# Activations' operands begin 0 to 128 bytes further into their places, by turns: linear attention and two squared-ReLU networks on one core

## The chip, the core and the metric

One core of a Trainium2 chip runs the whole program. The metric is device time in microseconds. The profile is of one execution; its times are us from the span's start.

## The reference, cut to what matters

```
q, k, v: 8 x 8 heads x 576 x 64
q_s = softmax(q) over the 64 features;  k_s = softmax(k) over the 576 positions
kv = k_s^T v  per head;   x = q_s kv    -> 4608 tokens x 512
for each of two networks (w_in 512 x 2048, w_out 2048 x 512):
    h = max(x @ w_in, 0);   x = (h * h) @ w_out
```

## The kernel before, in words

The tokens are worked in nine blocks j of 512; the 2048 hidden features are 16 blocks f of 128 (NF), or 8 pairs a (NPAIR), or 4 groups u of two pairs (NU). Every operand of a large matmul is kept as two halves of float32r, a high one and a low one (what the rounding left), and each product is three matmuls in a row, low x high, high x low, high x high: `passes`, line 460. Each matmul has a stationary operand of 128 columns, which is loaded anew for it, and a moving one of 512 or 256 columns.

There are four stages, one after the other:

1. The first network's first product, "h" (`h_mm`): 1728 matmuls of 512 columns. The weight w0 is stationary, the token block's x moving. Attention is done beside it: `attend(j, p)` for each of four pairs of heads p makes kv and x. x goes from the bank to memory in `x_hi` (L79, ScalarE, high half) and `x_lo` (L82, VectorE, low half). The result is taken out by `h_relu` (L447, ScalarE) and stored to HBM. A block of tokens is 16 hidden blocks of 12 matmuls, in order of the pair of heads c = 0 to 3, three matmuls for each.
2. Its second product, "y<-G,W" (`second`, l=0): 72 pairs (j, a) of 42 matmuls of 256 columns; G, the squared hidden values, is moving and the weight W stationary. Products are done in a form with 7 instead of 8 block products, whose operands are sums of blocks: `combine` makes them, by adds on VectorE or GpSimd (L100 to L104), the high half in `comb_hi` (L114, ScalarE) and the low half in `comb_lo` (L119, VectorE).
3. The second network's first product, "m<-x,W" (`first`): 36 units (j, u) of 84 matmuls; x moving, W stationary.
4. Its second product, "y<-W,G" (`second`, l=1): as stage 2, but W moving and G stationary.

Places in on-chip memory are laid out by hand, by `room` at the top, in the order of the calls; a room takes its words of four bytes, and at least 32 bytes. The rooms w0 to w7 hold the combined weights (14 x 256 words each), the rooms hl0 to hl3 the combined x and G; in the first stage w0 to w4 hold the weights w0 (three to a room, 1024 words each), hl0 and hl1 the x of even and odd token blocks for the pairs of heads 0 to 2, at words 1024 p, and hl3 ("ahead") holds the weight of hidden block 15 at word 0 and the x of pair 3 at word 1024 for even and 2048 for odd blocks. G of the last stage (names G1_...) begins SHIFT = 32 words into its place. At the start, the data of two pairs of heads lie in one room, 1738 words apart (`start_load`), and their transposes (`k_turn0`, `q_turn0`) take them as the stationary operand.

The order of all instructions on each engine comes from a planner (`schedule`) with costs and due times, which knows places by name and not by address; the eight banks of "ps" are given out in the order in which they come free. Waits between engines are added where the addresses that one instruction writes overlap what another reads or writes.

Of the kernel before, what the change touches and what calls it, by code (L numbers as in the profile page):

```python
# [16 lines left out]
B, H, S, D = 8, 8, 576, 64  # L17
# [4 lines left out]
NP = H // 2  # L22
TB = 512
HB = TB // 2
NB = NT // TB
NF = DFF // P
NPAIR = NF // 2
# [3 lines left out]
SHIFT = 32  # L31
# [12 lines left out]
def linear_attention_two_relu2_ffn(ctx: ExitStack, tc: tile.TileContext, q0, k0, eye, qh, kh, vh, wio, out):  # L44
# [15 lines left out]
    def room(tag, n):  # L60
        pool.tile([P, n], F32, name=f"{tag}_room", tag=tag)

    for i in range(8):
        room(f"w{i}", 14 * HB)
    for tag, n in (("kvn", D), ("qm", 16), ("qs", 16), ("qmo", 16)):
        room(tag, n)
    room("hl3", 14 * HB)
    room("hl0", 14 * HB + SHIFT)
    for tag, n in (("qso", 16), ("kvs", 1), ("kvm", 1), ("margin0", 64)):
        room(tag, n)  # L70
    room("hl1", 14 * HB + SHIFT)
    room("margin1", 96)
    room("hl2", 14 * HB + SHIFT)

    def f32(ap):
        return ap.bitcast(F32)
# [14 lines left out]
    hls, cfs = {}, {}  # L91


    def comb_add(key, q, x, eng, new):
# [8 lines left out]
        else:  # L103
            e.tensor_tensor(out=cf[:, 4], in0=q[:, 0], in1=q[:, 3], op=ALU.add)  # L104

    def comb_hi(key, q, x, tag):
        if key not in hls:
            if key.startswith("G1_"):
                t = pool.tile([P, 14 * HB + SHIFT], F32R, name=key, tag=tag)
                hls[key] = t[:, SHIFT:].rearrange("p (a b n) -> p a b n", a=2, b=7)  # L110
            else:
                hls[key] = pool.tile([P, 2, 7, HB], F32R, name=key, tag=tag)
        r, src = (slice(0, 2), q[:, 0:4:3]) if x == 0 else (slice(2, 7), cfs[key])
        nc.scalar.activation(out=hls[key][:, 0, r], in_=src, func=AF.Copy)  # L114
# [223 lines left out]
    kvn = {}  # L338
# [25 lines left out]
    qmo, qso = {}, {}  # L364
# [104 lines left out]
    m, t, t_place = {}, {}, {}  # L469
# [235 lines left out]
    def combine(key, tag, due, engines, q, place, after, cfplace, new):  # L705

        hl = Place(tag)
        n = (512, 512, 256)
        adds = [op(e, gps(n[x]) if e == "POOL" else dve(n[x]), due - 5200 + 10 * x, lambda x=x, e=e: comb_add(key, q(), x, e, new), after, [place, cfplace], port=True)
                for x, e in enumerate(engines)]  # L710
        h0 = op("ACT", act(512), due - 4500, lambda: comb_hi(key, q(), 0, tag), after, [hl, place])
        h1 = op("ACT", act(1280), due - 3000, lambda: comb_hi(key, q(), 1, tag), adds, [hl, cfplace])
        l0 = op("DVE", dve(512), due - 2500, lambda: comb_lo(key, q(), 0), [h0], [hl, place], port=True)
        l1 = op("DVE", dve(1280), due - 1500, lambda: comb_lo(key, q(), 1), [h1], [hl, cfplace], port=True)
        combined[key] = [l0, l1], hl
# [50 lines left out]
    ahead = Place("hl3")  # L766
# [94 lines left out]
    xspace = [Place("hl0"), Place("hl1")]  # L861

    def attend(j, p):
# [3 lines left out]
        if j == 0:  # L867
            room = start_places[p]
        kvnew = lambda: kp.area(0, KC * (P + 2 * (D + 1)))
        qnew = lambda: qspace.area(TB * (p % 2), TB)  # L870
        if own:
            ps = Place("ps")
            n, s = Place("kvn"), Place("kvs")
# [33 lines left out]
        else:  # L907
            q = Place(f"q{p % 2}", parent=qspace)
            lq = dma(d - 30000, lambda: load_q(j, p, qnew), 256, [], [q])
            qm, qo, qs, so, qT, qd = Place("qm"), Place("qmo"), Place("qs"), Place("qso"), Place("qT"), Place("qd")  # L910
# [15 lines left out]
                kv_ready[p] = op("DVE", 450, d - 5500, lambda: kv_lo(j, p), [hi], [n, kvp[p]], port=True)  # L926
                xlast = op("PE", 60 + 3 * 29 * (8 - j), d - 4500, lambda: x_mm(j, p, 1, xb), [kv_ready[p], xm], [xb, qd, kvp[p]], lag=SLACK)
        par = j % 2
        room2, lo = (ahead, 1024 * (1 + par)) if p == NP - 1 else (xspace[par], 1024 * p)
        xp = x_place[j, p] = Place(f"x{par}_{p}", parent=room2)  # L930
        y = op("ACT", act(512, 1), d - 2000, lambda: x_hi(j, p, lambda: part2(room2, lo)), [xlast], [xp, xb])
        x_ready[j, p] = op("DVE", dve(512), d - 1000, lambda: x_lo(j, p), [y], [xp, xb])
# [1 line left out]
    for j in range(NB):  # L934
        for p in range(NP):
            plan(when(0, j) - 25000 - (3 - p) * 12500, lambda j=j, p=p: attend(j, p))
# [246 lines left out]
```

## Time and profile before

| | |
|---|---|
| median of 3 runs | 1572.17 us (1571.39, 1572.17, 1589.4) |
| profiled execution | 1568.28 us, its span 1566.5 us |
| TensorE busy / weight loads busy | 1529.8 / 1428.7 us |
| VectorE, ScalarE, GpSimd busy | 1203.2, 957.8, 418.1 us |
| mean granted clock of TensorE | 0.992 |

The span is from the first to the last instruction. Matmuls overlap in the records: one of 256 columns lasts 276 to 281 ns, while the next begins some 115 ns after it. So the pace of a stretch is its length, less the last one's own duration where that is in it, by the number of intervals.

### The profile page before, as it was taken

The page shows a single profiled execution, that of the slowest core. Times are in us where ns is not written, and L with a number is a line of the kernel's source. Part 1 is how long each engine was busy: PE and PEld are TensorE (multiplying, and loading weights), DVE is VectorE, ACT ScalarE, POOL GpSimd, SP SyncE. Part 2 cuts the span into 40 slices and gives each one's busy share as a digit, 9 for nine tenths or more (in the row PEclk, how much of TensorE's full clock was granted, in tenths as well). Part 3 has the DMA queues.
Part 4 walks back from the last instruction along what each step waited for, and adds up shares of the span by engine and source line. Part 5 has one row for each costly group of instructions (what it writes and reads, how often), then busy time and mean ns, then how long its engine had stood idle before and what let it go on. Part 6 is the DMA issues. An engine that isn't in the chain of part 4 may idle for free.

```text
span 1566.5 us, 30005 instructions
## 1 busy us (share of the span) xinstructions
PE 1529.8 (98%) x11664; PEld 1428.7 (91%) x11664; DVE 1203.2 (77%) x1758; ACT 957.8 (61%) x1605; POOL 418.1 (27%) x337
## 2 busy tenths in 40 slices
PE   6899999999999999999999999999999899999998
PEld 4678878878888999999999999999999899999998
DVE  7897887778744888888889855555445898999987
ACT  7666765667655655555555788888777444444442
POOL 1010000000013233333323444333321433334332
PEclk9899999999999999999999999999999999999999
DMA  8447766778685444444437667767648544444432
GB/s 327 155 140 219 252 226 211 230 266 274 242 293 178 139 146 134 135 135 136 135 109 250 239 213 248 242 224 241 209 169 292 206 137 146 136 142 141 136 118 85
DMA packets 143103, 299.86 MB, mean 191 GB/s; under 512 B 12528, under 2 KB 72048, under 8 KB 141424
## 3 DMA queue, kind: packets, MB, share of 16 engines
q1 hardware_dynamic: 141808, 283.26, 54.4%
q0 software_dynamic: 1152, 14.68, 2.5%
q8 instruction: 91, 1.49, 0.4%
q14 instruction: 52, 0.43, 0.1%
HBM read 176.26 MB, written 121.63 MB: 190 GB/s over the span
## 4 chain that ended last, share of the span: by engine, by line
PE 91%; DVE 3%; DMA 2%; ACT 2%; issue 1%; POOL 0%; SPq 0%; DVEq 0%; ACTq 0%; POOLq 0%
PE y L460 42%; PE h L460 25%; PE m L460 20%; PE kvps L329 2%; DMA g<-t 1%; DMA hl<-g 1%; PE xps L422 1%; PE xps L423 1%; PE xps L424 1%; DVE G L119 0%; DMA w<-k 0%; DMA raw<-wio 0%; ACT w L147 0%; DVE w L82 0%; POOL att L104 0%
## 5 line engine op out<-in xcount | busy, mean ns | idle before, releaser
L460 PE MATMUL h<-hl,w 128*128 128x512 f32 x1620 | 402.2, 403 | 10.2 <-DVE w L82 10.2
L460 PEld LDWEIGHTS h<-hl,w 128*128 128x128 f32 x1620 | 305.6, 191 | 83.9 <-DVE w L82 9.6
L460 PE MATMUL y<-G,W 128*128 128x256 f32 x3024 | 356.5, 281 | 1.1 <-DVE G L119 1.1
L460 PEld LDWEIGHTS y<-G,W 128*128 128x128 f32 x3024 | 356.3, 189 | 1.3 <-DVE G L119 1.3
L460 PE MATMUL y<-W,G 128*128 128x256 f32 x3024 | 346.1, 277 | 4.1 <-DVE G L119 4.1
L460 PEld LDWEIGHTS y<-W,G 128*128 128x128 f32 x3024 | 345.5, 189 | 4.5 <-DVE G L119 4.5
L460 PE MATMUL m<-x,W 128*128 128x256 f32 x3024 | 343.5, 276 | 0.1
L460 PEld LDWEIGHTS m<-x,W 128*128 128x128 f32 x3024 | 343.1, 188 | 0.3 <-ACT ts L493 0.3
L114 ACT ACTIVATE G<-hl 128x512 fp32r<-128x512 f32 (+1 forms) x106 | 93.1, 889 | 139.2 <-PE y L460 82.6
L119 DVE TENSOR_TENSOR G<-hl,G 128x512 fp32r<-128x512 f32 (+1 forms) x106 | 129.6, 1228 | 20.4 <-ACT G L114 20.4
L447 ACT ACTIVATE r<-h 128x512 f32<-128x512 f32 x144 | 85.6, 595 | 84.2 <-PE h L460 79.1
L496 POOL TENSOR_TENSOR ts<-ts,ts 128x512 f32<-128x512 f32 x53 | 83.3, 1571 | 160.2 <-ACT ts L493 156.2
L314 POOL PARTITION_ALL_REDUCE m<-m x28 | 25.4, 908 | 348.2 <-DVE m L310 168.9
L511 ACT ACTIVATE t<-t 128x512 f32<-128x512 f32 x144 | 90.2, 631 | 3.6
L119 DVE TENSOR_TENSOR G<-cf,G 128x1280 fp32r<-128x1280 f32 x51 | 85.9, 1683 | 6.3 <-ACT G L114 6.3
L505 DVE TENSOR_TENSOR t<-m,ts 128x512 f32<-128x512 f32 x72 | 48.7, 688 | 53.0 <-PE m L460 36.8
L119 DVE TENSOR_TENSOR G<-att,G 128x1280 fp32r<-128x1280 f32 x50 | 81.8, 1637 | 7.6 <-ACT G L114 7.5
L114 ACT ACTIVATE G<-qc 128x512 fp32r<-128x512 f32 x41 | 25.9, 632 | 79.1 <-PE y L460 65.5
L114 ACT ACTIVATE G<-qd 128x512 fp32r<-128x512 f32 x40 | 25.3, 632 | 79.1 <-PE y L460 51.7
L114 ACT ACTIVATE G<-att 128x1280 fp32r<-128x1280 f32 x50 | 63.3, 1266 | 15.2 <-DVE att L102 12.0
L114 ACT ACTIVATE G<-cf 128x1280 fp32r<-128x1280 f32 x51 | 64.6, 1266 | 11.4 <-DVE cf L102 8.2
L538 POOL TENSOR_TENSOR t<-t,t 128x512 f32<-128x512 f32 x34 | 62.5, 1859 | 30.1 <-DVE t L505 30.1
(175 smaller groups left out, 1977.4 us busy)
## 6 DMA issues: line engine op xcount, KB each, us to landing
g<-r SPq DMA_DIRECT2D x144, 256.0 KB, 3.4
g<-t SPq DMA_DIRECT2D x144, 256.0 KB, 3.5
hl<-g SPq DMA_DIRECT2D x63, 512.0 KB, 3.7
raw<-wio SPq DMA_DIRECT2D x48, 512.0 KB, 5.0
qc<-g SPq DMA_DIRECT2D x41, 512.0 KB, 3.8
qd<-g SPq DMA_DIRECT2D x40, 512.0 KB, 3.7
y<-t SPq DMA_DIRECT2D x72, 256.0 KB, 2.3
W<-o POOLq DMA_DIRECT2D x8, 1792.0 KB, 9.7
```

Of the source, the lines that this page charges most:

```text
L114: nc.scalar.activation(out=hls[key][:, 0, r], in_=src, func=AF.Copy)
L119: nc.vector.tensor_tensor(out=hl[:, 1, r], in0=src, in1=f32(hl[:, 0, r]), op=ALU.subtract)
L314: nc.gpsimd.partition_all_reduce(m[:, 1, :P], m[:, 0, :P], P, bass.bass_isa.ReduceOp.max)
L329: nc.tensor.matmul(ps[j * D:(j + 1) * D, 0:D + 1], k[lo:, c, j * D:(j + 1) * D], v[lo:, c, j, :], start=(c == 0), stop=(c == KC - 1),)
L422: nc.tensor.matmul(ps[:, r], w[:, 1], q[:, 0, r], start=True, stop=False)
L423: nc.tensor.matmul(ps[:, r], w[:, 0], q[:, 1, r], start=False, stop=False)
L447: nc.scalar.activation(out=r0[j, f].rearrange("p a b -> p (a b)"), in_=m.pop(("h", j, f)), func=AF.Relu)
L460: nc.tensor.matmul(ps, a, b, start=start, stop=True, skip_group_check=True)
L496: nc.gpsimd.tensor_tensor(out=t[k, "s5"], in0=t[k, "s5"], in1=t[k, "s2"], op=ALU.add)
L505: nc.vector.tensor_tensor(out=temp(k, q), in0=m[k, i], in1=t[k, "s5"], op=ALU.add)
L511: nc.scalar.activation(out=t[k, q], in_=t[k, q], func=AF.Square)
L538: nc.gpsimd.tensor_tensor(out=t[k, q], in0=t[k, q], in1=t[k, o], op=ALU.add)
```

## The change

The moving and stationary operands that are made of x and G no longer all begin at the start of their places (or 32 words in, for G1). A new function `further` gives the words: for G of layer l, token block j, pair a it is 4 x ((8 j + a) modulo 9), for x{j}_{kk} of the second network 4 x j, and the first stage's x begins 4 j words further too. So the starts go through 0, 16, ... 128 bytes. The weights' places stay. The rooms hl0 to hl3 all have 32 words more than the operand needs, and the small rooms between them are laid out anew, so that the hl rooms lie 14592 bytes apart; kvn has no room of its own at this point any more and comes later.

```diff
-    for tag, n in (("kvn", D), ("qm", 16), ("qs", 16), ("qmo", 16)):
+    for tag, n in (("qm", 16), ("qs", 16), ("kvs", 1)):
         room(tag, n)
-    room("hl3", 14 * HB)
-    room("hl0", 14 * HB + SHIFT)
-    for tag, n in (("qso", 16), ("kvs", 1), ("kvm", 1), ("margin0", 64)):
-        room(tag, n)
-    room("hl1", 14 * HB + SHIFT)
-    room("margin1", 96)
-    room("hl2", 14 * HB + SHIFT)
+    for i, between in ((3, (("qmo", 16), ("qso", 16))), (0, (("kvm", 1), ("margin0", 24))), (1, (("margin1", 32),)), (2, ())):
+        room(f"hl{i}", 14 * HB + SHIFT)
+        for tag, n in between:
+            room(tag, n)
...
+    def further(key):
+
+        n = [int(x) for x in key[1:].split("_")]
+        return 4 * ((n[1] * NPAIR + n[2]) % 9 if key[0] == "G" else n[0])
+
     def comb_hi(key, q, x, tag):
         if key not in hls:
-            if key.startswith("G1_"):
+            if key[0] in "Gx":
                 t = pool.tile([P, 14 * HB + SHIFT], F32R, name=key, tag=tag)
-                hls[key] = t[:, SHIFT:].rearrange("p (a b n) -> p a b n", a=2, b=7)
+                o = further(key)
+                hls[key] = t[:, o:o + 14 * HB].rearrange("p (a b n) -> p a b n", a=2, b=7)
...
-        room2, lo = (ahead, 1024 * (1 + par)) if p == NP - 1 else (xspace[par], 1024 * p)
+        room2, lo = (ahead, 1024 * (1 + par) + 4 * j) if p == NP - 1 else (xspace[par], 1024 * p + 4 * j)
```

## Rows read from the trace of the kernel before

**Rows 1.** The page's busy times: engine, us, share of the span, instructions.

```profile
PE 1529.8 (98%) x11664; PEld 1428.7 (91%) x11664; DVE 1203.2 (77%) x1758; ACT 957.8 (61%) x1605; POOL 418.1 (27%) x337
```

**Rows 2.** The page's chain that ended last: shares by engine, by line.

```profile
PE 91%; DVE 3%; DMA 2%; ACT 2%; issue 1%; POOL 0%; SPq 0%; DVEq 0%; ACTq 0%; POOLq 0%
PE y L460 42%; PE h L460 25%; PE m L460 20%; PE kvps L329 2%; DMA g<-t 1%; DMA hl<-g 1%; PE xps L422 1%; PE xps L423 1%; PE xps L424 1%; DVE G L119 0%; DMA w<-k 0%; DMA raw<-wio 0%; ACT w L147 0%; DVE w L82 0%; POOL att L104 0%
```

**Rows 3.** The same chain in order of time: start, length, engine, count.

```profile
457.54 53.10 PE h L460 x228
510.64 336.39 PE y L460 x2856
...
872.23 315.82 PE m L460 x2784
...
1235.32 323.58 PE y L460 x2838
```

**Rows 4.** Windows, line 460: length, PE and PEld busy (count), clock, DMA.

```profile
520.00:840.00 320.00, 320.00 (x2719) 320.00 (x2718) 1.00 0.41 134
...
1240.00:1540.00 300.00, 300.00 (x2649) 300.00 (x2648) 1.00 0.41 133
...
468.00:507.00 39.00, 39.00 (x168) 31.42 (x168) 1.00 0.62 193
```

**Rows 5.** Timeline of PE around the pause at 863 us.

```profile
855.33 5.82 PE L460 MATMUL y<-G,W 128*128 128x256 f32 x48
...
865.13 2.66 PE L460 MATMUL y<-G,W 128*128 128x256 f32 x22
```

**Rows 6.** Timeline of PE, beginning of the last stage.

```profile
1208.28 2.99 PE L460 MATMUL y<-W,G 128*128 128x256 f32 x24
```

**Rows 7.** Timeline of PE, end of the first stage.

```profile
507.73 2.23 PE L460 MATMUL h<-hl,hl 128*128 128x512 f32 x9
509.80 0.84 PE L460 MATMUL h<-hl 128*128 128x512 f32 x3
510.48 0.28 PE L460 MATMUL y<-G,W 128*128 128x256 f32 x1
```

**Rows 8.** Timeline of PE, q times kv of block 4.

```profile
244.72 0.28 PE L422 MATMUL xps<-qhl,kvbd 128*128 128x256 f32 x1
244.84 0.28 PE L423 MATMUL xps<-qhl,kvbd 128*128 128x256 f32 x1
```

**Rows 9.** Timeline of PE, transposes of the start, pairs 2 and 3.

```profile
15.31 0.60 PE L273 MATMUL ka<-begin,w 128*128 128x128 f32 x4
...
16.71 0.60 PE L273 MATMUL ka<-begin,w 128*128 128x128 f32 x4
```

**Rows 10.** Timeline of several engines around the ends of blocks 3, 5, 7.

```profile
259.80 0.69 DVE L82 TENSOR_TENSOR hl<-xps,hl 128x512 fp32r<-128x512 f32 x1
260.81 2.73 PE L460 MATMUL h<-hl,w 128*128 128x512 f32 x11
...
363.65 0.69 DVE L82 TENSOR_TENSOR hl<-xps,hl 128x512 fp32r<-128x512 f32 x1 [0.28 <-ACT hl L79]
365.43 0.40 PE L460 MATMUL h<-hl,w 128*128 128x512 f32 x1
...
458.21 0.69 DVE L82 TENSOR_TENSOR hl<-xps,hl 128x512 fp32r<-128x512 f32 x1
460.92 1.26 ACT L114 ACTIVATE S<-cf 128x1280 fp32r<-128x1280 f32 x1
465.73 3.67 PE L460 MATMUL h<-hl,w 128*128 128x512 f32 x15
```

**Rows 11.** The page's groups and DMA issues that write or read activations.

```profile
L114 ACT ACTIVATE G<-qc 128x512 fp32r<-128x512 f32 x41 | 25.9, 632 | 79.1 <-PE y L460 65.5
...
hl<-g SPq DMA_DIRECT2D x63, 512.0 KB, 3.7
...
qc<-g SPq DMA_DIRECT2D x41, 512.0 KB, 3.8
```

## The prediction, made before the result was known

> **What bounds the kernel now.** I read the page's busy table first: TensorE is busy 98% of the span, and the weight loader 91% beside it [rows 1]. The chain of work that ended last says the same from the other side: 91% of the span is TensorE, 87% the three matmul groups of the two networks, and no wait of another engine takes more than about 1% [rows 2]. So only two things can move the time: the interval from one matmul to the next, and a wait that newly reaches TensorE. VectorE and ScalarE at 77% and 61% are cover.
>
> The interval is then to be read stage by stage, from unbroken stretches of the chain [rows 3], since the table of groups gives mean durations that overlap. It is the length divided by the count: 53.10/228 = 232.9 ns for the 512-column matmuls of the first network's first product (h), 336.39/2856 = 117.8 ns for its second product (y, 256 columns), 315.82/2784 = 113.4 ns for the second network's first (m), 323.58/2838 = 114.0 ns for its second. The granted clock is 1.00 in the stretches looked at [rows 4], its 2.4 GHz level, so one column per cycle would be 213.3 and 106.7 ns. All lie above that, and two stages with the same shape differ by 4 ns without a clock to explain it.
>
> The useful view is the timeline of TensorE around pauses. At 855 us y<-G,W runs at (5.82-0.28)/47 = 117.9 ns (0.28 is the last one's own duration, the last row of [rows 7] shows one alone). After a pause near 863 the very same product runs at (2.66-0.28)/21 = 113.3 [rows 5]. Then m keeps the fast one (its 113.4) for over 300 us; the next stage starts at 1208 us with (2.99-0.28)/23 = 117.8, and from 1240 us it holds 300/2649 = 113.3 [rows 3, 4, 6]. So 256-column matmuls with the same relation of addresses have two stable paces, about 113.3 and 117.8, entered by chance after a disturbance and held for hundreds of us. In this profile y got the slow one, m and nearly all of the last stage the fast one. The three times of the kernel spread by 18 us; one stage in the other pace is 3024 x 4.5 ns = 13.6 us, which is the right size.
>
> Does the address matter at all? One place speaks for it. From the layout, all weights of the stages begin on one residue modulo 512 bytes, and each moving or stationary activation so that the weight-side operand lies 64 bytes ahead (modulo 512): the room hl3 begins 448 bytes (modulo 512) behind the weights' room, the spacings between the hl rooms are multiples of 512, and G of the last stage, there the stationary one, has the extra 128. Only the weight w0 of hidden block 15 lies in hl3 itself, with distance 0 from x. There h runs at 226.7 ns: three matmuls from 509.80 until the next stage starts at 510.48 [rows 7], against 232.9 beside it. It isn't clean: the nine before these take (2.23-0.39)/8 = 230, as if the pace settled over some matmuls. In 4 and 8 ns steps, then, relative position seems to matter, and 113.3 and 226.7 (17/16 of a cycle per column) look like the floor.
>
> **The change part by part.** No instruction is added, removed or reordered, so I cost four things.
>
> (1) *New relations.* The hl rooms now begin 160 bytes behind the weights modulo 256, and each operand 16k further, k from 0 to 8. The stationary operand's lead over the moving one, 64 before, becomes 96-16k (96 down to -32, modulo 256) in the first three stages, and -96+16k in the last. x has k = j through a whole token block; G of the second products has a new k for each of the 72 pairs of hidden blocks. No row shows any lead but 64, 0 and those of a few short products, so this is bounded. From below by the floor: 113.3 and 226.7. From above by the slow pace that lasts, 117.8, and for h by 232.9. Further away, 256-column matmuls of the q times kv product (distance 0) follow one another at 120 ns [rows 8], but these come three at a time after other work; I take 120 as the far end alone. Between floor and slow pace I take the middle, 115.6 and 229.8: nothing in the rows prefers one end, each was entered from a restart, and nine relations in turn make it unlikely that a stage stays in one.
> - y: 3024 x (115.6-117.8) = -6.7 us
> - m: 3024 x (115.6-113.4) = +6.7 us
> - last stage: 3024 x (115.6-114.0) = +4.8 us
> - h: 1728 x (229.8-232.9) = -5.4 us
>
> Sum -0.6 us.
>
> The Trainium skill, in "TensorE: Matmul & The Clock Gate" (Part 2, Step-by-step: what each phase is for), says that TensorE has two independent read ports, so that loading the next weights takes nothing from the running matmul. By it the relation of addresses would be worth nothing and (1) would be 0 instead of -0.6 us; the 226.7 beside 232.9 is against it, weakly, and it is a rival below.
>
> (2) *Starts that are no multiple of 64 bytes.* The transposes of the start are such a case, with the data as the stationary operand: in one room pair 3's k lies 6952 bytes (40 modulo 64) behind pair 2's, and groups of four take 0.60 us for both, (0.60-0.27)/3 = 110 ns an interval [rows 9]. So an unaligned start of weights costs under 1 ns. For a moving operand I see no row at full pace; 0, at most 1 ns on 10,800 matmuls (11 us, inside the bounds of (1)).
>
> (3) *A new wait.* The x of head pair 3 lies in hl3 at word 1024+4j for even j and 2048+4j for odd j. For even j the end of its low half at 2048+4j now covers the first four words of the previous block's x, at 2048+4(j-1). So x_lo (L82, VectorE) has to wait for the last matmul of block j-1. For j=2 that had ended anyway. For j=4 it ran at 259.80 and the next block began at 260.81; for j=6 at 363.65 against 365.43; for j=8 at 458.21 against 465.73 [rows 10]. VectorE will stand 1.0, 1.8 and 7.5 us. Behind it at j=8 are adds for a weight that is kept, and ScalarE's conversion of their sums (460.92) then holds back h_relu, which empties TensorE's banks. I cost it at nothing: x_lo's 0.69 us end by 466.5, and the matmul that reads it is the eleventh of the block, 10 x 0.233 us after its start, at 468.1; ScalarE is held some 7 us, or three hidden blocks at 2.8 us, and there are eight banks, handed out in turn; the next product starts only at 510. Without that cover it costs the waits themselves, 10.3 us together.
>
> (4) *Other engines.* Their operands move too, by whole 16 bytes. I take nothing: their work lies beside TensorE, with ScalarE idle for longer before its conversions of G (79.1 us in 41) than they take (25.9), and loads into hl land in 3.7 us, into qc in 3.8 [rows 11], 20 us ahead of use. A loss of 5% on these would still be covered.
>
> The profiled run took 1568.28 us, 3.9 below the median of 1572.17. Its sum gives 1567.7; on the median, 1571.6.
>
> **The rivals.**
> - *All released to the floor* (the slow pace is a lock that needs a fixed relation; changing it by turns breaks it). y 3024 x 4.5 = 13.6, h 1728 x 6.2 = 10.7, the others 2.4: 26.7 us, so 1546. For: the pause at 863 cleared it, and distance 0 gave the floor in h. Against: at 1208 the fast pace was lost as easily.
> - *Slow throughout, the other side* (each turn of the relation knocks the matmuls into 117.8). m +13.3, last stage +11.5: 1597, and 1600 with part of (3). It decides from the point where more than half of the 256-column matmuls run slow. For: the changes from fast to slow around 1208. Against: there matmuls of two products alternated, and G's changes come only every 42.
> - *Slower than any lasting pace shown*: 256 columns at 120, h 3.1 ns above its 232.9: 9072 x (120-115.1) + 1728 x 3.1 = 50 us, 1622. For: rows 8. Against: no long stretch does that.
> - *The change does nothing*: pace is TensorE's own, entered by chance. Then the middle of before, 1572, with its own spread up to 1589.
> - *The 17/16 goes too*: 9072 x 6.6 + 1728 x 13.4 = 83 us below the floor case at most, half of it 1505. Against: it is the same at distance 0 and 64.
>
> **How the numbers follow.** The forecast (a mixture) has 0.47; a quarter to three quarters slow gives +-10.1 us for the 256s and +-2.7 for h, 1559 to 1585. Released 0.15, slow throughout 0.20, slower than shown 0.10, nothing 0.05, floor gone 0.03. The time is the mixture's, 1571. Its range reaches to 1546 and to 1600, the bounds of (1), and leaves out the two far cases, 0.13. Two per cent, about what a measurement here can tell from no change, is 31 us: faster only with the floor gone, 0.03; slower with 120 ns, or slow with every wait of (3) uncovered (1607), 0.12; the rest 0.85.
>
> **What would show it.** In the chain of the changed kernel: the mean interval of each stage, against 115.6, 115.6, 115.6 and 229.8; in windows by token block, steps of h and m with j (one relation each), which would prove that address and not chance sets the pace; stretches of hundreds of us at one pace across many k would prove the rival that nothing hangs on it. On VectorE, x_lo of blocks 4, 6 and 8 ending 0.7 us after the block boundary, and no pause of TensorE behind it. The prediction is wrong if some leads cost much more than 4.5 ns, or if TensorE pauses near 466 us.

## The result, and the profile after

The changed kernel takes 1594.95 us, median of 4 runs (1594.16 to 1596.04), against 1575.25 for the kernel before in the same job; the ratio is 1.0113, 95% interval 1.0066 to 1.0159. It is slower, by less than the 2% bound and by more than the interval. It lies inside the range, 24 us above the forecast, at the rival "slow throughout" (1597). The profiled execution took 1596.04 us, its span 1594.2, so 27.7 more than the span before.

The page first: busy table, then the chain that ended last, by engine (answers to rows 1 and 2).

```profile
PE 1556.9 (98%) x11664; PEld 1454.8 (91%) x11664; DVE 1204.2 (76%) x1758; ACT 957.8 (60%) x1605; POOL 415.5 (26%) x337
...
PE 76%; DVE 1%; DMA 1%; POOL 1%; issue 1%; ACT 0%; DVEq 0%; POOLq 0%; ACTq 0%; SPq 0%
```

TensorE gained 27.1 us of busy time with the same 11664 matmuls; the other engines moved by less than 3 us, and the mean granted clock is 0.992 in both executions. (In this trace the chain couldn't be followed back over the first 300 us; the shares add to 80%.) So the time is in the matmuls themselves. The chain in order of time says in which (start, length, what; answers to rows 3):

```profile
331.58 5.67 PE h L463 x24
...
397.29 5.47 PE h L463 x24
...
457.79 53.11 PE h L463 x228
510.90 331.82 PE y L463 x2814
...
869.51 353.35 PE m L463 x3000
...
1249.56 337.08 PE y L463 x2838
```

| stage | ns a matmul before [rows 3] | after | forecast |
|---|---|---|---|
| h, 512 columns | 232.9 | 53.11/228 = 232.9 (last blocks) | 229.8 |
| y | 117.8 | 331.82/2814 = 117.9 | 115.6 |
| m | 113.4 | 353.35/3000 = 117.8 | 115.6 |
| last | 114.0 | 337.08/2838 = 118.8 | 115.6 |

By these rates m costs 3024 x 4.4 = 13.3 us more and the last stage 3024 x 4.8 = 14.5. The starts of the stages in the two traces (y 510.48 and 510.74, m 867.85 and 869.35, last stage 1208.28 and 1222.69) share the 27.7 out exactly: 0.3 before y, 1.2 in y, 12.9 in m, 13.3 from the last stage on, which had run its first matmuls at 117.8 before the change too [rows 6].

The lead is how far the stationary operand's start lies ahead of the moving one's, modulo 256 bytes. The first two rows of h show that blocks with different leads do differ: 236 ns in block 5 (lead 16), 228 in block 6 (lead 0).

The view that tells most is the timeline of TensorE inside m, where each token block has one lead for about 40 us. Rows: start, length, group, count; the interval is (length - 0.28)/(count - 1).

```profile
874.74 27.50 PE L463 MATMUL m<-x,W 128*128 128x256 f32 x233
...
911.79 30.45 PE L463 MATMUL m<-x,W 128*128 128x256 f32 x254
...
956.83 25.44 PE L463 MATMUL m<-x,W 128*128 128x256 f32 x223
...
991.75 30.43 PE L463 MATMUL m<-x,W 128*128 128x256 f32 x254
...
1071.82 30.39 PE L463 MATMUL m<-x,W 128*128 128x256 f32 x258
...
1111.77 30.40 PE L463 MATMUL m<-x,W 128*128 128x256 f32 x252
...
1151.80 30.42 PE L463 MATMUL m<-x,W 128*128 128x256 f32 x255
```

Block 0, lead 96: 117.3 ns. Block 1, lead 80: 119.2. Block 2, lead 64: 113.3. Block 3, lead 48: 119.2. Block 5, lead 16: 117.2. Block 6, lead 0: 120.0. Block 7, lead -16: 118.6. (Blocks 4 and 8, leads 32 and -32, ran at 118.3 and 116.7.) One of the nine relations is as fast as before, the one that the kernel before had everywhere; the others all cost 3 to 7 ns. The short turns of y repeat it (last three rows: pairs at leads 80, 64, 48 of token block 2, 119.5, 113.1, 119.2). But not every turn at lead 64 was fast: of its eight in y, one (first row, token block 1) stayed at 117.8 to its end.

```profile
565.49 4.52 PE L463 MATMUL y<-G,W 128*128 128x256 f32 x37
...
605.23 4.82 PE L463 MATMUL y<-G,W 128*128 128x256 f32 x39
...
610.71 4.24 PE L463 MATMUL y<-G,W 128*128 128x256 f32 x36
...
615.02 4.81 PE L463 MATMUL y<-G,W 128*128 128x256 f32 x39
```

The new wait, in the timeline of VectorE and TensorE at the ends of blocks 3, 5 and 7 (answers to rows 10; in brackets the idle time before and its releaser):

```profile
259.90 2.27 PE L463 MATMUL h<-hl,w 128*128 128x512 f32 x9
260.17 0.69 DVE L79 TENSOR_TENSOR hl<-xps,hl 128x512 fp32r<-128x512 f32 x1 [0.93 <-PE h L463]
...
366.64 1.54 PE L463 MATMUL h<-hl,w 128*128 128x512 f32 x6
366.91 0.69 DVE L79 TENSOR_TENSOR hl<-xps,hl 128x512 fp32r<-128x512 f32 x1 [3.36 <-PE h L463]
...
460.68 0.69 DVE L79 TENSOR_TENSOR hl<-xps,hl 128x512 fp32r<-128x512 f32 x1 [2.36 <-PE h L463]
465.96 0.85 PE L463 MATMUL h<-hl,w 128*128 128x512 f32 x3
```

VectorE stands 0.9, 3.4 and 2.4 us, and TensorE goes from block to block without a pause, as costed. The third one is let go 5 us before the block's end: x_lo of block 8 stands in the program ahead of block 7's hidden blocks 14 and 15, so it waits for 13 alone. Those two hidden blocks then read four columns of block 7's x (pair of heads 3, high half) that already hold block 8's; the changed kernel computes that part of four tokens otherwise than the reference, and so do the runs below that keep this place of x (lead 0 fixed, lead 64 fixed, h alone). It changes no duration.

### The profile page after: what moved, and what is told of

Its sections match the earlier page's. It is cut to its first block, busy times and chain, and to the rows that moved or that the text cites. A ratio compares the mean times of both kernels' runs of the same rounds, so it can differ in the third digit from the quotient of the medians.

```text
span 1594.2 us, 30008 instructions
## 1 busy us (share of the span) xinstructions
PE 1556.9 (98%) x11664; PEld 1454.8 (91%) x11664; DVE 1204.2 (76%) x1758; ACT 957.8 (60%) x1605; POOL 415.5 (26%) x337
## 4 chain that ended last, share of the span: by engine, by line
PE 76%; DVE 1%; DMA 1%; POOL 1%; issue 1%; ACT 0%; DVEq 0%; POOLq 0%; ACTq 0%; SPq 0%
PE y L463 43%; PE m L463 22%; PE h L463 10%; DMA qc<-g 0%; PE kvps L332 0%; DVE G L122 0%; DMA hl<-g 0%; POOL cf L101 0%; ACT G L117 0%; POOL att L101 0%; PE xps L426 0%; PE xps L427 0%; PE xps L425 0%; ACT qc L457 0%; DVEq L1182 0%
## 5 line engine op out<-in xcount | busy, mean ns | idle before, releaser
L463 PE MATMUL y<-W,G 128*128 128x256 f32 x3024 | 359.8, 281 | 3.8 <-DVE G L122 3.8
L463 PEld LDWEIGHTS y<-W,G 128*128 128x128 f32 x3024 | 359.1, 189 | 4.2 <-DVE G L122 4.2
L463 PE MATMUL m<-x,W 128*128 128x256 f32 x3024 | 356.6, 280 | 0.0
L463 PEld LDWEIGHTS m<-x,W 128*128 128x128 f32 x3024 | 356.4, 189 | 0.0
```

The lines of the kernel that those rows point to most:

```text
L463: nc.tensor.matmul(ps, a, b, start=start, stop=True, skip_group_check=True)
```

## The experiments

Theory: the value of the lead, modulo 256, sets the pace (the interval between matmuls), at lead 64 with two possible paces. Rivals: that the turning costs (each new relation disturbs the lock), that starts off a multiple of 64 bytes cost, or that only the lead modulo 128 counts. One thing no run separates for y, m and the last stage: the weights there always begin on one residue, so "lead" could also be read as the place of the activation's own start. Only in h did the weights move.

**One lead for y and m: 0, then 64.**

```diff
-        return 4 * ((n[1] * NPAIR + n[2]) % 9 if key[0] == "G" else n[0])
+        return 4 * ((n[1] * NPAIR + n[2]) % 9) if key.startswith("G1") else 24     # 8 for lead 64
```

> The changed kernel, but x and G of the first network have one fixed shift of 96 bytes, so the stationary operand leads the moving one by 0 (modulo 256) through all of y and m; h and the last stage stay as changed. If the value of the lead sets the pace: 119.9 ns in y and m (what the changed kernel shows at lead 0), 1606 us. If the turning costs (each new relation disturbs the matmuls): one lead throughout, so 113.3 in both, 1568 us. If starts off a multiple of 64 bytes cost: these are on one, so 113.3 too, 1568 us.

> As the one before, but fixed at a shift of 32 bytes: lead 64 through y and m. If the value of the lead sets the pace: 113.3 in m and y, or 117.8 where the second of the two paces of lead 64 is entered, never 119.9; 1568 us with both fast, 1581 with one of them. If the turning costs: 113.3 in both, 1568. If starts off a multiple of 64 bytes cost: these start at 64 modulo 128, so 113.3. Beside the kernel at lead 0 it tells the lead from the rest.

Measured 1609.15 and 1573.23 us, one run each. The chain of the first:

```profile
511.42 337.70 PE y L463 x2814
...
875.69 360.00 PE m L463 x3000
```

The timeline of TensorE of the second, y and m:

```profile
519.73 320.44 PE L463 MATMUL y<-G,W 128*128 128x256 f32 x2826
...
869.78 315.46 PE L463 MATMUL m<-x,W 128*128 128x256 f32 x2781
```

120.0 ns in both stages at lead 0, 113.3 in both at lead 64. Nothing turns in either, and both start on multiples of 64 bytes: neither of those rivals can make the difference, and the order and the layout of rooms are the same, so nothing else of the change is behind it. 2 x 3024 x 6.7 = 40 us expected between them, 36 measured.

**Lead 64 against 192, all starts as aligned as before.**

```diff
-            if key.startswith("G1_"):
+            if key[:2] == "G0" or key[0] == "x":
```
(in the kernel before; hl3 gets the 32 words too, and the margins keep the spacings of the rooms at multiples of 256 bytes).

> The kernel before, with x and G of the first network 128 bytes further and G of the second not: the lead is -64 (192 modulo 256) in y, m and the last stage, fixed, every start on a multiple of 64; h as before. If the lead modulo 256 sets the pace: 117.7 in all three (the changed kernel's 192 in its last stage), 1597 us. If only the lead modulo 128 counts: as before, 113.3 or 117.8 by stage, 1559 to 1589. If unaligned starts or the turning cost: 113.3 or 117.8 as before.

Measured 1596.24 us (one run). Its chain:

```profile
513.93 336.39 PE y L461 x2856
...
871.41 353.33 PE m L461 x3000
...
1250.78 336.06 PE y L461 x2838
```

117.8, 117.8 and 118.4 (with the pauses inside). By itself this doesn't show that the period isn't 128, since 117.8 is also the slow pace of lead 64, and all three stages could have entered it; the map below shows it. That the period is 256 and not more shows in the changed kernel's block 2 of m, whose two x lie in rooms 256 bytes apart modulo 512 and ran as one stretch at 113.3.

**A map of leads.** The rooms have 256 bytes to spare and all begin on one residue modulo 256, and the first stage's x lies as in the kernel before; only the function is shown.

```diff
+        if key[0] == "x":
+            return n[0]
+        x = n[1] * NPAIR + n[2]
+        return 4 * (x % 16) if n[0] == 0 else x % 64
```

> A map of leads: rooms with 256 bytes to spare, G of the first network in 16 steps of 16 bytes (all leads), x of the second stage's blocks at leads 64, 60, ... 32, G of the last stage in 64 steps of 4 bytes; the first stage's x as before, at lead 64. If the value sets the pace: units of equal lead agree in all rounds of the turn and between stages; 113.3 at 64, 119.9 at 0, 116.5 to 119.5 at 16 to 48, 80, 96, 192 to 240; the new ones 112 to 176 between 113.3 and 120; total 1585 to 1600 us. If the turning costs: all units alike, near 118, whatever their lead. In 4-byte steps nothing new within 16 bytes if lines of 16 bytes count, a smooth curve if not.

Measured 1610.08 us (one run). The timeline of TensorE, in y at leads 16, 0 and 144, in the last stage at 76, 80, 88 and 144, and in m's block 0 at lead 64:

```profile
767.95 4.02 PE L464 MATMUL y<-G,W 128*128 128x256 f32 x33
...
772.76 4.12 PE L464 MATMUL y<-G,W 128*128 128x256 f32 x33
...
807.78 3.79 PE L464 MATMUL y<-G,W 128*128 128x256 f32 x32
...
1419.38 4.13 PE L464 MATMUL y<-W,G 128*128 128x256 f32 x35
...
1424.30 4.08 PE L464 MATMUL y<-W,G 128*128 128x256 f32 x33
...
1434.07 4.13 PE L464 MATMUL y<-W,G 128*128 128x256 f32 x35
...
1503.06 4.84 PE L464 MATMUL y<-W,G 128*128 128x256 f32 x39
...
874.83 34.44 PE L464 MATMUL m<-x,W 128*128 128x256 f32 x291
```

In y 116.9 at lead 16, 120.0 at 0, 113.2 at 144; in the last stage 113.2 at 76 and 88, 118.8 at 80. Leads 16 and 144 agree modulo 128 and differ by 3.7 ns, so the period isn't 128. Four bytes decide: the neighbours of 76 and 88 are at 118 to 120, so it is no matter of lines of 16 bytes.

My expectation had units of equal lead agreeing between the stages, and in this it failed, as its 1585 to 1600 us did: lead 144 is at 113.2 in y and at (4.84-0.28)/38 = 120.0 in the last stage, where the other operand moves. The lead alone isn't enough, then.

And the last row is the second thing to learn: lead 64 for the whole block at (34.44-0.28)/290 = 117.8. Lead 64 has a second pace.

**Lead 64 in all three stages, then 88.**

```diff
-        return 4 * ((n[1] * NPAIR + n[2]) % 9 if key[0] == "G" else n[0])
+        return 0 if key.startswith("G1") else 32      # 88: 6 and 26
```
(rooms: only qm ahead of hl3, 128 bytes behind each hl room, so that 0 and 128 bytes give lead 64 in all stages; in h x as in the change at lead 96-16j, for 88 at 64.)

> The changed kernel with fixed shifts in y, m and the last stage that make the lead 64 in all three (rooms laid out for it); h still by turns, 96 down to -32 by token block. If the value of the lead sets the pace: 113.3 in all three, 1559 us (the run with lead 64 in y and m, less 3024 x 4.7 ns in the last stage); 13 us more for each stage that enters the slow pace of lead 64, so 1559, 1572 or 1585. If the gain of that run came from something else in y and m, the last stage stays at 118.

> As before it, but lead 88 in y, m and the last stage and 64 throughout h, as in the kernel before. 88 is no multiple of 16 or 64. If the value of the lead sets the pace: 113.4 in all three as in the map's unit at 88 (which got there within two matmuls), 1560 us. If only multiples of 64 (or of 16) are good: 117 to 120 in all three, 1595 to 1610. If 88 has a slow pace too, one entered by chance: 1572 to 1590 and runs that differ by 13 us.

Lead 64: 1562.11 us, median of 6 runs, ratio 0.9937 (0.9895 to 0.9979) to the kernel before. Timeline of y and m, then the chain's row of the last stage:

```profile
519.83 319.19 PE L461 MATMUL y<-G,W 128*128 128x256 f32 x2815
...
869.82 315.38 PE L461 MATMUL m<-x,W 128*128 128x256 f32 x2780
...
1228.27 323.54 PE y L461 x2838
```

113.3, 113.4 and 114.0 with its pauses: every stage in the fast pace, 33 us below the changed kernel. (Five of the six runs lie within 4 us; the sixth took 1573.32.) Lead 88: 1594.68 us, median of 4, ratio 1.0135 (1.0092 to 1.0178). Its chain:

```profile
510.25 337.24 PE y L461 x2814
874.82 360.00 PE m L461 x3000
...
1260.39 323.81 PE y L461 x2838
```

119.8 and 120.0 with the activations moving, 114.0 with the weights moving. So the map's good row at 88 held for the last stage alone, and my expectation of 1560 was wrong: the same lead has a fast pace and a slow one here as well, or it matters which operand moves, or where each operand starts and not the difference alone. Which of these was not tried. For the second or third speak lead 144 in the map, good in one stage and bad in the other, and that the four runs at 88 all took 1593 us or more.

**A map for h.** The x shifted by 15 words for each token block, w0 by 3 for each room of three hidden blocks.

> As the run at lead 88, but in h the x shifted by 60 bytes for each token block and the weights by 12 bytes for each room of three hidden blocks, so that h passes through 49 leads in stretches of 36 matmuls. If the value of the lead sets the pace in h too: 227 to 229 ns at 0, 233 at 64, 236 at 16, and others between 226.7 and 237; the mean near 233, so h as long as before (480 us). If h doesn't hang on it: 233 in every stretch. y, m and last stage at lead 88 again, entered from elsewhere: 113.4 if that pace is firm.

1594.64 us (one run), h as long as before. Timeline of TensorE in h, leads 244 and 64:

```profile
289.38 5.61 PE L461 MATMUL h<-hl,w 128*128 128x512 f32 x24
...
444.68 7.59 PE L461 MATMUL h<-hl,w 128*128 128x512 f32 x31
```

(5.61-0.39)/23 = 227.0 and (7.59-0.39)/30 = 240.0, at a lead that ran at 233 before: h too hangs on the operands' starts, 227 to 240. One lead has more than one pace here too; but the starts themselves differ between the two runs, so this may be the starts and not the entry. y and m came out at 120 once more.

**h at lead 0, and h alone.** The run with lead 64, but w0 lies 16 words further and x at the start of its place, so h is at lead 0 in blocks 0 to 7 (x 8 words further and lead -32 in block 8). And the kernel before with the last line of the change only (shown):

```diff
-        room2, lo = (ahead, 1024 * (1 + par)) if p == NP - 1 else (xspace[par], 1024 * p)
+        room2, lo = (ahead, 1024 * (1 + par) + 4 * j) if p == NP - 1 else (xspace[par], 1024 * p + 4 * j)
```

> The run with lead 64 in y, m and the last stage, and in h lead 0 for token blocks 0 to 7 (its weights 64 bytes further), -32 for block 8. If the value of the lead sets the pace in h as well: 229 instead of 233.3 ns there, 1536 x 4.3 ns = 6.6 us less than the run at lead 64, 1555 us. If y falls into its slow pace because of what h ends with: 1569. If h is bound by something else there: 1562.

> The kernel before with one part of the change alone: the first stage's x begins 4 j words further (leads 64 down to -64), and with it the wait of the low half on the block before. y, m and last stage at lead 64 as before. If the turns in h or that wait cost anything, h gets longer than 479.5 us and the time rises above the kernel before. If not, h stays within 3 us of it, VectorE stands 1 to 4 us at three block ends, and the rest is as before: 1560 with y fast, 1573 with y slow.

The first: 1577.22 us, median of 12 (1566.78 to 1587.96), ratio 0.9980 (0.9940 to 1.0019). Timeline of a stretch of h at lead 0, then the chain:

```profile
428.18 11.04 PE L461 MATMUL h<-hl,w 128*128 128x512 f32 x48
...
504.42 331.44 PE y L461 x2814
...
864.95 353.33 PE m L461 x3000
...
1244.25 324.58 PE y L461 x2838
```

h did what was expected, (11.04-0.39)/47 = 226.6 ns, and y began at 504.3 instead of 508.9. But in the profiled execution y and m fell into 117.8 at the very lead, 64, that had run at 113.3, and lost 27 us; the 12 runs of this one program spread over 21 us. The second: 1570.95 us, median of 10 (1561.19 to 1584.87), ratio 0.9936 (0.9896 to 0.9975). Its chain:

```profile
510.13 318.94 PE y L460 x2814
856.50 335.81 PE m L460 x2856
1235.82 324.68 PE y L460 x2838
```

y at 113.3 for once, m at 117.6, of the same addresses as the kernel before, which had them the other way round [rows 3]. h took 478.7 us (31.27 to 509.97) against 479.5: this part of the change, wait included, costs nothing. So the addresses of y and m don't decide which of the two paces they enter. What does isn't shown by these two runs: the same program gives both from one execution to the next.

**A push into the fast pace.** The changed kernel came to lead 64 from lead 80 in its turn, and was mostly fast after a few matmuls (in seven of eight turns of y within 6, in m after some 26; the expectation counts more generously). So the run with h at lead 0, and a stretch at lead 80 where a stage or token block begins:

```diff
-        return 0 if key.startswith("G1") else 32
+        kick = n[-1] == 0 if key[0] == "G" else n[0] == 0
+        return 4 * kick if key.startswith("G1") else 32 - 4 * kick
```

> The run with h at lead 0, and the first pair of each token block in y and in the last stage, and the whole first token block in m, at lead 80 instead of 64: a stretch at another lead just before lead 64 begins. If the two paces of lead 64 are a matter of how it is entered (the changed kernel came to 64 from 80 in its turn, and was fast within six matmuls in 9 of 10 such places): 113.3 in y, m and last stage but for those stretches at 119, 336 x 5.8 ns = 1.9 us in each of the three, 1561 us, and runs closer together than the 21 us of the kernel without it. If the slow pace is entered by chance at any time: as that one, 1567 to 1588.

1561.42 us, median of 6 (1557.41 to 1564.56), ratio 0.9883 (0.9837 to 0.9928): faster than the kernel before by less than the 2% bound and more than the interval, and 33.5 us below the changed kernel, which ran in another job. Timeline of y after its first push, of m after its first block, and of the last stage ahead of its second push, then the last stage's row of the chain:

```profile
508.06 32.14 PE L462 MATMUL y<-G,W 128*128 128x256 f32 x282
...
899.75 290.42 PE L462 MATMUL m<-x,W 128*128 128x256 f32 x2561
...
1226.79 15.47 PE L462 MATMUL y<-W,G 128*128 128x256 f32 x130
...
1221.63 304.50 PE y L462 x2646
```

113.4, 113.3 and 115.1 (with pushes and pauses). The third row is a control inside the run: after two pauses, of 2.1 and 3.4 us, the last stage was at (15.47-0.28)/129 = 117.8, at lead 64, until the next push brought it back to 113.3. In this execution all 19 pushes were followed by the fast pace. Nothing in the program but those stretches differs from the run at 1577 (ratios to the kernel before in the same job 0.988 and 0.998), so the two paces of lead 64 in y, m and the last stage are a matter of entry, and entry can be steered. Whether it takes lead 80, or any other lead would do, was not tried. Nor is the push needed for the time: the run with lead 64 in all stages reached 1562.11 without it, at a slower h. There the last token block of h ran at lead -32 as here, all but its last hidden block, and y was still entered fast; so what spoils an entry stays unknown.

## Why the prediction was wrong

**The step that failed** is in (1), the middle between floor and slow pace, 115.6, because "nothing in the rows prefers one end". The nine leads aren't draws between the two paces of lead 64: each has a pace of its own, and eight of nine lie at 116.7 to 120 in m. The upper bound failed too: I put 120 aside as a far end seen in threes only, and it is the lasting pace of lead 0 (1111.77 above, and 360.00/3000 with lead 0 fixed). Rows 8, the only ones at lead 0 with 256 columns, had told it; I took 226.7 in h at lead 0 as the sign that 0 is good, and what is best of those seen for 512 columns is worst for 256.

By its terms: y +0.3 instead of -6.7, m +13.3 instead of +6.7, last stage +14.5 instead of +4.8, h 0 instead of -5.4 (block 5, at lead 16, was 1.8 us longer than before; blocks 6 and 7, at 0 and -16, 1.0 shorter together). The last stage's 14.5 is by its rate; its length grew by 13.3. The rival "slow throughout" had m +13.3 and last +11.5 and gave 1597, which the result met by luck; its mechanism, turns knocking the matmuls into the slow pace, was not the right one, since a fixed lead is as slow (117.8 at 192, 120.0 at 0).

**What held.** The reading that two paces exist at one lead, entered after pauses and at the starts of stages and held for hundreds of us: the map, the run with h alone and the push show it, and that the times of the kernel before spread by 18 us fits (the changed kernel's four lie within 2, and lead 64 is one turn in nine there). That addresses matter at all, weakly argued from rows 7, is shown. The Trainium skill's sentence that TensorE's two read ports are independent ("TensorE: Matmul & The Clock Gate", Part 2, Step-by-step: what each phase is for) would leave the lead worth nothing, and these runs are against that: lead 0 against 64 alone is 6.7 ns of 113.3. (2) held as well: the last stage's stationary operand at 88 bytes, no multiple of 64, ran at 114.0, and a moving one at 112 (lead 144 in y) at 113.2. (3) cost nothing; its third wait was 2.4 us and not 7.5, for the order of the program. (4) held too: ScalarE was busy for 957.8 us as before, VectorE for 1204.2 against 1203.2.

**What stays open.** Why those leads are good: no run here shows it. Whether 88 is slow and 144 fast in y by entry, by which operand moves, or by the starts themselves; for that, the weights would have to move in those stages. And what decides the entry into lead 64 without a push.

## What to carry to other kernels

Where TensorE is the bound and weights are loaded for each matmul, look at the interval between matmuls by stretch, and at the difference of the two operands' addresses: here it was worth 6% of a stage, with no instruction changed. Keep one measured good lead rather than spread over many; and where a profile shows two paces for the same work, try what comes just before each, for that can be chosen. An effect seen with one shape didn't carry to another here: measure the lead for each width and for each operand that moves.

## What the runs showed of the hardware

- 256-column float32r matmuls with a weight load each: 113.3 to 120.0 ns, by the lead modulo 256 bytes and the stage, at a granted clock of 0.99 to 1.00; 512 columns: 226.6 to 240.
- At one lead more than one lasting pace: 113.3 or 117.8 at 64, held over 3000 matmuls; a stretch of 42 matmuls at lead 80 before it (336 in m) brought the fast one.
- 113.3 and 226.6 are 17/16 of a cycle a column at 2.4 GHz; no run got below.
